# The fifth key piece: a DMA transpose on ScalarE's queue in place of a load, five TensorE transposes and a copy

## The chip, the core and the metric

The kernel runs on one core of one Trainium2 chip. The metric is the device time of one execution in microseconds (us); lower is better. Three executions of the kernel before took 236.49, 236.51 and 236.56 us.

## The reference

The kernel computes one transformer block on x of 1 x 2048 tokens x 640 channels, all in bf16: a linear attention with a learned feature map (32 heads of 20 channels), then a feed-forward layer of 1728 hidden channels. Both have a layer norm ahead of them and a residual around them.

```python
qkv = (x @ wqkv) -> q, k, v                       # x here is layernorm(x)
pq = einsum("bhsd,hdf->bhsf", q, w_phi)           # pk likewise, from k
phi_k = concat(softmax(pk), softmax(-pk))         # phi_q likewise
kv = einsum("bhsf,bhsd->bhfd", phi_k, v);  z = sum_s phi_k
o = einsum(phi_q, kv) / (einsum(phi_q, z) + 1e-6)
h = x + o @ wo
h2 = h + silu(layernorm(h) @ w1) @ w2
```

## The kernel before, in words

The 2048 tokens are 16 tiles of 128. Weights stay in on-chip memory; the 640 input channels are five pieces of 128 rows (C = 5).

The kernel never computes k and then pk. It folds the key weights and `w_phi` into one matrix `Wfk` (640 x 640) first, so that one projection gives pk. Folding contracts over the output channels of the key weights, so TensorE needs their transpose `wTk`, piece by piece. For each piece c of the key weights, before the change:

- `lk` loads it (128 rows x 640 columns, 160 KB) into `wk[:, c]` (the DMA is issued at L236, in the helper `dma`);
- `wt.c` (L322) transposes its five 128 x 128 blocks on TensorE into one bank of PSUM;
- `wc.c` copies them to `wTk` (L171 on ScalarE for pieces 0 and 1, L169 on VectorE for pieces 2, 3 and 4);
- `fk.c` (L337) multiplies that piece of `wTk` by `phb`, the block-diagonal form of `w_phi`, in six matmuls;
- `fc.c` (L171, a cast) copies the result to `Wfk[:, c]` on ScalarE.

Beside this, the first tiles of x are made ready. `st` (L273, L274) takes mean and variance on VectorE; `rs` (L278 on VectorE, then L281 and L283 on GpSimd) turns the variance into a reciprocal root, L281 being the power; `xn` (L297) normalizes on VectorE; `xt` (L308) transposes on TensorE and `xc` copies the result to `XnT`. Then `kp.0` (L370), the first projection by `Wfk`, starts the long row of matmuls that lasts to the end.

Before the first key piece is there, TensorE runs matmuls on constants (`wm`, L268): eight of 512 columns ahead of `wt.0`, six of 256 columns between `wt.0` and `wt.1`.

The order on every engine is written out by hand in one long string, `ORDER`: each word calls one operation, and each engine runs its instructions in the order of the words. A letter `s` behind a load puts the DMA on SyncE's queue, `a` on ScalarE's, `@n` names the PSUM bank. The loads of the key pieces 0 to 3 are on SyncE's queue, that of piece 4 is the third and last DMA on ScalarE's queue, behind x tile 0 and `w_phi`. The completion semaphores of the DMAs go round among eight; a DMA that gets a semaphore again waits on its queue until the DMA that had it before has landed. Here the load of x tiles 4 to 7 (`lx.4.8`, on SyncE's queue) gets the semaphore of piece 4.

The kernel already holds DMA transposes: `xd`, `td` and `hd` (L315, L559, L630) move normalized tiles through them, and `lq` (L251) brings the five pieces of the query weights in transposed from DRAM, all on SyncE's queue. The first of these is issued 16.37 us after the start.

Of the kernel before, what the change touches and what calls it, by code (L numbers as in the profile page):

```python
# [22 lines left out]
WHERE = {t: (g, i) for g, ts in enumerate(GROUPS) for i, t in enumerate(ts)}  # L23

ORDER = """
mk mo lx.0.1.a lk.0.1.s lp.a lx.1.2.s lk.4.5.a wm.512@7 wm.512@7 wm.512@7 wm.512@7 wm.512@7 wm.512@7
wm.512@7 wm.512@7 wt.0@0 lk.1.2.s ta wc.0.a wm.256@2 wm.256@2 wm.256@2 wm.256@2 wm.256@2 wm.256@2 wt.1@1 wc.1.a st.0 rs.0.1
ph.v fk.0@2 fc.0.a st.1 lk.2.3.s wt.2@4 wc.2.v lk.3.4.s wt.3@5 wc.3.v fk.1@6 fc.1.a rs.1.2 fk.2@0 fc.2.a
lx.2.4.s xn.0.v lx.8.12.s wt.4@4 wc.4.v lv.0.3.s fk.3@2 fc.3.a xt.0@5 xn.1.v xc.0.v st.2 fk.4@6 fc.4.a
rs.2.3 lv.3.5.s mc.0 xt.1@4 xc.1.a st.9 st.8 rs.8.10 lx.4.8.s st.3 rs.3.4 kp.0@0 ke.0 xn.2.a kp.1@2 ke.1  # L30
lx.12.16.s vp.1@6 st.10 xt.2@5 vp.0@0 xc.2.a xn.9.a vc.0.a vp.2@2 st.11 lo.2.5.s xn.3.v xt.3@4 xc.3.a
rs.10.12 xn.8.a vc.2.a vc.1.a kp.2@0 ke.2 st.4 xd.9 st.5 kp.3@4 lo.0.2.s ke.3 rs.4.6 vp.3@2 xn.11.v vp.9@6
# [38 lines left out]
def kernel(  # L71
# [11 lines left out]
    nc = tc.nc  # L83

    P = nc.NUM_PARTITIONS
    T = 16
    D = 640
# [46 lines left out]
    wTk = first.tile([P, C, D], BF16, name="wTk")  # L134
# [116 lines left out]
        nc.sync.dma_start_transpose(wTq[:, :, c * P : (c + 1) * P], A_wqkv[c * P : (c + 1) * P, 0:D])  # L251

    def op_lt(c, q="s"):
        nc.sync.dma_start_transpose(wTk[:, :, c * P : (c + 1) * P], A_wqkv[c * P : (c + 1) * P, D : 2 * D])

    def op_lo(a, b, q="s"):
        dma(q, wo[:, a:b, :], A_wo[a * P : b * P].rearrange("(c p) n -> p c n", p=P))
# [500 lines left out]
```

## Time and profile before

| | before |
|---|---|
| median of 3 runs | 236.51 us (236.49 to 236.56) |
| profiled execution, whole | 236.35 us |
| its span in the profile | 234.4 us |
| granted TensorE clock | 1.0 |
| TensorE busy | 230.5 us, 98% of the span |
| VectorE / ScalarE / GpSimd busy | 133.5 / 114.5 / 95.4 us |

The span runs from the first to the last instruction that the profiler records; 1.95 us of the profiled execution lie outside it. In the views, PE is TensorE's matmuls and PEld its weight loads, DVE is VectorE, ACT ScalarE, POOL GpSimd, SP SyncE; a "q" behind a name (SPq, ACTq) is the engine's queue of issued DMAs and waits. A row of the timeline gives the start in us, the time that it took in us, the engine, the line of the code, the operation, output<-input, how many, and in brackets the idle time before it and what ended it.

### The profile page before, as it was taken

To read this page: it belongs to the slowest core of one execution; us is meant where nothing else is said; L and a number is where in the kernel's file an instruction comes from. 1 tells how busy PE (TensorE), PEld (TensorE's weight loads), DVE (VectorE), ACT (ScalarE), POOL (GpSimd) and SP (SyncE) were. 2 spreads that over 40 slices of the span, in tenths; PEclk is the share of its full clock that TensorE was granted. 3 is DMA by queue.
4 is the path that set the end of the run, shared out by engine and by line. 5 is a ranking of instruction groups with operands and counts; after the bars stand their busy time and mean duration, and the time that the engine had idled before them with its cause. 6 is when DMAs were issued, how large, how long until landed. Compare 5 with 4: busy or idle time off the path is not lost.

```text
span 234.4 us, 6307 instructions
## 1 busy us (share of the span) xinstructions
PE 230.5 (98%) x2674; PEld 148.4 (63%) x2674; DVE 133.5 (57%) x249; ACT 114.5 (49%) x171; POOL 95.4 (41%) x190
## 2 busy tenths in 40 slices
PE   8999999999999999999999999999999999999995
PEld 4777777776554556876645455556776865566662
DVE  3999999999968899788956641301341310001132
ACT  3789996885857776742244536260040015613000
POOL 7485798997904455765285123141040000000000
PEclk9999999999999999999999999999999999999999
DMA  7967758839101375325823202123212300000112
GB/s 203 381 234 147 82 112 110 182 64 350 37 3 31 59 176 148 59 49 98 142 55 61 56 3 55 30 57 63 88 24 57 106 27 5 0 3 2 54 34 81
DMA packets 44844, 20.67 MB, mean 88 GB/s; under 512 B 34448, under 2 KB 44304, under 8 KB 44816
## 3 DMA queue, kind: packets, MB, share of 16 engines
q1 hardware_dynamic: 43728, 19.88, 36.1%
q10 hardware_dynamic: 1088, 0.39, 0.8%
q8 instruction: 21, 0.34, 0.6%
q14 instruction: 7, 0.06, 0.1%
HBM read 9.61 MB, written 2.62 MB: 52 GB/s over the span
## 4 chain that ended last, share of the span: by engine, by line
PE 98%; ACT 1%; DVE 0%; issue 0%
PE mm L691 24%; PE mm L645 24%; PE mm L370 19%; PE mm L457 10%; PE mm L566 9%; PE mm L504 3%; PE mm L268 2%; PE mm L427 2%; PE mm L337 1%; PE mm L655 1%; PE mm L704 1%; ACT EqT L479 1%; PE mm L322 1%; PE mm L308 0%; DVE ob L721 0%
## 5 line engine op out<-in xcount | busy, mean ns | idle before, releaser
L691 PE MATMUL mm<-w,shT 128*128 128x320 bf16 (+2 forms) x416 | 58.7, 299 | 0.0
L645 PE MATMUL mm<-HnT,w 128*128 128x512 bf16 (+1 forms) x325 | 58.6, 337 | 0.0
L691 PEld LDWEIGHTS <-shT 128*128 128x128 bf16 x416 | 39.6, 98 | 17.2 <-issue 1.1
L667 ACT ACTIVATE shT<-mm 128x1024 bf16<-128x1024 f32 (+2 forms) x29 | 27.6, 963 | 44.6 <-PE mm L645 43.1
L712 DVE TENSOR_TENSOR ob<-mm,X 128x640 bf16<-128x640 f32 x15 | 12.3, 819 | 62.3 <-PE mm L691 59.3
L645 PEld LDWEIGHTS <-w 128*128 128x128 bf16 x325 | 31.4, 98 | 23.2
L370 PEld LDWEIGHTS <-XnT 128*128 128x128 bf16 x320 | 30.8, 98 | 12.0
L414 POOL TENSOR_TENSOR Ek<-Ek,Sk 128x1280 bf16<-128x1280 bf16 (+2 forms) x15 | 32.9, 2217 | 4.0 <-DVE Sk L406 4.0
L539 POOL TENSOR_TENSOR o<-u,rd 128x320 bf16<-128x320 f32 x28 | 19.9, 727 | 22.9 <-DVE rd L533 16.4
L583 ACT ACTIVATE sq<-X 128x640 bf16<-128x640 bf16 x16 | 11.7, 732 | 28.3 <-DVE X L575 27.2
L566 PE MATMUL mm<-wo,ot 128*128 128x320 bf16 x160 | 23.9, 299 | 0.3 <-ACT EqT L479 0.3
L457 PE MATMUL mm<-XnT,Wfq 128*128 128x512 bf16 x100 | 23.8, 380 | 0.0
L370 PE MATMUL mm<-wv,XnT 128*128 128x320 bf16 x160 | 23.7, 299 | 0.0
L370 PE MATMUL mm<-Wfk,XnT 128*128 128x320 bf16 x160 | 23.5, 299 | 0.0
L395 ACT ACTIVATE Ek<-mm 128x640 bf16<-128x640 f32 x32 | 20.5, 714 | 6.0 <-PE mm L370 5.1
L403 DVE TENSOR_REDUCE Sk<-Ek 128x64 f32<-128x1280 bf16 x16 | 23.2, 1452 | 0.3 <-ACT Ek L395 0.3
L479 ACT ACTIVATE EqT<-mm 128x1024 bf16<-128x1024 f32 (+1 forms) x24 | 19.7, 879 | 4.9 <-PE mm L457 4.8
L575 DVE SCALAR_TENSOR_TENSOR X<-mm,X 128x640 bf16<-128x640 f32 x16 | 13.0, 818 | 15.4 <-PE mm L566 15.1
L566 PEld LDWEIGHTS <-ot 128*128 128x128 bf16 x160 | 15.7, 98 | 7.3 <-issue 0.2
L273 DVE BATCH_NORM_STATS2 stats<-X 128x6 f32<-128x320 bf16 x32 | 13.6, 467 | 3.8 <-DMA X<-in_A_x_dram 3.8
L457 PEld LDWEIGHTS <-Wfq 128*128 128x128 bf16 x100 | 9.1, 98 | 9.3
L525 DVE TENSOR_TENSOR u<-mm,w 128x672 f32<-128x672 f32 x16 | 13.7, 857 | 1.2 <-DVE w L523 0.3
(78 smaller groups left out, 204.3 us busy)
## 6 DMA issues: line engine op xcount, KB each, us to landing
out_dram<-ob SPq DMA_DIRECT2D x15, 160.0 KB, 1.8
w<-in_B_w_dram SPq DMA_DIRECT2D x6, 360.0 KB, 4.5
X<-in_A_x_dram SPq DMA_DIRECT2D x3, 640.0 KB, 7.8
w<-in_B_w_dram SPq DMA_DIRECT2D x5, 320.0 KB, 5.8
wk<-in_A_wqkv_dram SPq DMA_DIRECT2D x4, 160.0 KB, 4.2
wv<-in_A_wqkv_dram SPq DMA_DIRECT2D x1, 480.0 KB, 6.4
wo<-in_A_wo_dram SPq DMA_DIRECT2D x1, 480.0 KB, 9.7
w<-in_B_w_dram SPq DMA_DIRECT2D x1, 480.0 KB, 4.6
```

The lines of the kernel that those rows point to most:

```text
L370: nc.tensor.matmul(ps[:, half, 0:320], tok(XnT[t // GT], t)[:, c, :], W[:, c, half * 320 : (half + 1) * 320], start=(c == 0), stop=(c == C ...
L395: nc.scalar.activation(Ek[:, s, :].rearrange("p (a n) -> p a n", a=2), tl["kp", t][:, :, 0:320], AF.Exp, scale=1.0 - 2.0 * s,)
L403: nc.vector.tensor_reduce(Sk[:], tl["ek", t][:].rearrange("p s (h f) -> p (s h) f", f=DH), axis=AX.X, op=ALU.add,)
L414: nc.gpsimd.tensor_tensor(Ek3[:, 0:n], Ek3[:, 0:n], Sk[:, 0:n].unsqueeze(2).to_broadcast([P, n, DH]), op=ALU.mult,)
L457: nc.tensor.matmul(tl["qp", g, i][:, k, :], Wfq[:, c, r * P : (r + 1) * P], XnT[g][:, c, :], start=(c == 0), stop=(c == C - 1),)
L479: nc.scalar.activation(E[:, s, rs[0] : rs[-1] + 1, :], tl["qp", g, i][:, 0 : len(rs), :], AF.Exp, scale=1.0 - 2.0 * s,)
L525: nc.vector.tensor_tensor(u[:], A[1][:, :, :, 0:21], w[:].unsqueeze(3).to_broadcast([P, 4, 8, 21]), op=ALU.mult,)
L539: (nc.vector if eng == "v" else nc.gpsimd).tensor_tensor(tl["o", t][:, a * 320 : (a + 1) * 320].rearrange("p (h f) -> p h f", f=DH), tl["u ...
L566: nc.tensor.matmul(ps[:, half, 0:320], tl["ot", t][:, c, :], wo[:, c, half * 320 : (half + 1) * 320], start=(c == 0), stop=(c == C - 1),)
L645: nc.tensor.matmul(ps[:, i * W : (i + 1) * W], w1[:, c, fc * P : (fc + 1) * P], HnT[g][:, c, 0:W], start=(c == 0), stop=(c == C - 1), skip ...
L667: nc.scalar.activation(sh[:, a:b], tl["up", g, k][:, 0 : b - a], AF.Silu)
L691: nc.tensor.matmul(ps, shT[g][:, fc * W + i * P : fc * W + (i + 1) * P], w2[:, fc, a:b], start=first and fc == 0, stop=last and fc == FC - ...
```

## The change

Piece 4 is no longer loaded into `wk`. A DMA transpose on ScalarE's queue, at the place of the former load, writes its transpose from DRAM straight into `wTk`. The load of the piece, its five transposes on TensorE (`wt.4`) and its copy on VectorE (`wc.4`) go. `op_lt` was in the kernel before, but no word of `ORDER` called it; it now takes the queue. Everything else keeps its place: `fk.4` stands where it did, now waiting for the DMA in place of the copy.

```diff
-mk mo lx.0.1.a lk.0.1.s lp.a lx.1.2.s lk.4.5.a wm.512@7 wm.512@7 ...
+mk mo lx.0.1.a lk.0.1.s lp.a lx.1.2.s lt.4.a wm.512@7 wm.512@7 ...
...
-lx.2.4.s xn.0.v lx.8.12.s wt.4@4 wc.4.v lv.0.3.s fk.3@2 fc.3.a xt.0@5 xn.1.v xc.0.v st.2 fk.4@6 fc.4.a
+lx.2.4.s xn.0.v lx.8.12.s lv.0.3.s fk.3@2 fc.3.a xt.0@5 xn.1.v xc.0.v st.2 fk.4@6 fc.4.a
...
     def op_lt(c, q="s"):
-        nc.sync.dma_start_transpose(wTk[:, :, c * P : (c + 1) * P], A_wqkv[c * P : (c + 1) * P, D : 2 * D])
+        (nc.sync if q == "s" else nc.scalar).dma_start_transpose(wTk[:, :, c * P : (c + 1) * P], A_wqkv[c * P : (c + 1) * P, D : 2 * D])
```

Engine by engine: TensorE has ten rows fewer (five weight loads, five transposes), VectorE one copy fewer, ScalarE a transposing DMA issue in place of a plain one. The instructions of GpSimd and SyncE and their order are the same.

More of the change, by code (lines that the diff above doesn't have):

```diff
@@ L25 @@
 ORDER = """
-mk mo lx.0.1.a lk.0.1.s lp.a lx.1.2.s lk.4.5.a wm.512@7 wm.512@7 wm.512@7 wm.512@7 wm.512@7 wm.512@7
+mk mo lx.0.1.a lk.0.1.s lp.a lx.1.2.s lt.4.a wm.512@7 wm.512@7 wm.512@7 wm.512@7 wm.512@7 wm.512@7
 wm.512@7 wm.512@7 wt.0@0 lk.1.2.s ta wc.0.a wm.256@2 wm.256@2 wm.256@2 wm.256@2 wm.256@2 wm.256@2 wt.1@1 wc.1.a st.0 rs.0.1
 ph.v fk.0@2 fc.0.a st.1 lk.2.3.s wt.2@4 wc.2.v lk.3.4.s wt.3@5 wc.3.v fk.1@6 fc.1.a rs.1.2 fk.2@0 fc.2.a
-lx.2.4.s xn.0.v lx.8.12.s wt.4@4 wc.4.v lv.0.3.s fk.3@2 fc.3.a xt.0@5 xn.1.v xc.0.v st.2 fk.4@6 fc.4.a
+lx.2.4.s xn.0.v lx.8.12.s lv.0.3.s fk.3@2 fc.3.a xt.0@5 xn.1.v xc.0.v st.2 fk.4@6 fc.4.a
 rs.2.3 lv.3.5.s mc.0 xt.1@4 xc.1.a st.9 st.8 rs.8.10 lx.4.8.s st.3 rs.3.4 kp.0@0 ke.0 xn.2.a kp.1@2 ke.1
```

## The prediction

> **What bounds the kernel now.** I read the page's busy times and its chain first, then TensorE's waits, then the chain of the first 25 us, and last the timeline and the DMA landings of that stretch.
>
> ```profile
> PE 230.5 (98%) x2674; PEld 148.4 (63%) x2674; DVE 133.5 (57%) x249; ACT 114.5 (49%) x171; POOL 95.4 (41%) x190
> PE 98%; ACT 1%; DVE 0%; issue 0%
> PE mm L566 <- ACT EqT L479: 0.3, 1, 0.3
> ```
>
> TensorE is the bound from end to end: 98% busy, 98% of the chain, and once started its one long wait is 0.3 us. Little can absorb a shift of its row of matmuls, so what counts is when that row begins: the first projection, L370. The chain ahead of it:
>
> ```profile
> 6.25 0.45 PE mm L322 x5
> 6.70 0.32 PE mm L337 x6
> 7.02 0.56 PE mm L322 x10
> 7.58 0.80 PE mm L337 x12
> 8.37 0.28 PE mm L322 x5
> 8.65 0.32 PE mm L337 x6
> 8.96 0.28 PE mm L308 x5
> 9.24 0.48 PE mm L337 x6
> 9.72 0.32 PE mm L308 x5
> 10.04 4.19 PE mm L370 x30
> ```
>
> The chain is drawn as TensorE alone, because its modelled ends touch. The five transposes that the change removes stand in it at 8.37 with 0.28 us. Whether they are worth that much, the timeline tells: it shows which waits end just before TensorE's steps.
>
> ```profile
> 6.25 0.28 PEld L322 LDWEIGHTS <-wk 128*128 128x128 bf16 x5 [0.51 <-DMA wk<-in_A_wqkv_dram]
> 6.80 0.60 PEld L322 LDWEIGHTS <-wk 128*128 128x128 bf16 x10
> 7.33 0.89 DVE L169 COPY wTk<-mm 128x640 bf16<-128x640 bf16 x2 [0.22 <-PE mm L322]
> 8.14 0.14 DVE L278 TENSOR_SCALAR RS<-MV 128x1 f32<-128x1 f32 x1
> 8.37 0.67 POOL L281 TENSOR_TENSOR RS<-RS,nhalf 128x1 f32<-128x1 f32 x1 [1.52 <-DVE RS L278]
> 8.69 0.49 DVE L169 COPY wTk<-mm 128x640 bf16<-128x640 bf16 x1
> 9.10 0.44 DVE L297 TENSOR_SCALAR xn<-X,MV,RS 128x640 bf16<-128x640 bf16 x1
> 9.23 0.31 PEld L337 LDWEIGHTS <-wTk 128*128 128x128 bf16 x6 [0.16 <-DVE wTk L169]
> 9.45 0.48 DVE L169 COPY XnT<-mm 128x640 bf16<-128x640 bf16 x1
> 9.98 3.92 PEld L370 LDWEIGHTS <-XnT 128*128 128x128 bf16 x30
> ```
>
> Read backwards. The projection begins at 9.98, right after VectorE's copy of the first transposed tile (9.45 + 0.48 = 9.93). In program order that copy stands behind the second normalization (9.10). This one needs the power on GpSimd, which ends at 8.37 + 0.67 = 9.04. The power needs L278 at 8.14, which stands behind the copies of pieces 2 and 3 (7.33), these wait for piece 2's transposes on TensorE (weights from 6.80), and those run behind piece 1's, which wait for a DMA until 6.25. So the stretch from 6.25 to 9.98 hangs on the landing of key piece 1 and then runs through VectorE and GpSimd; from 8.2 on TensorE only looks like the bound.
>
> **What goes.** Five transposes (0.28 us) and the copy of 0.49 us, with TensorE's wait of 0.16 us for that copy. On the face of it 0.28 + 0.16 = 0.44 us of TensorE. But with the copy gone VectorE is free from 8.69 on and then stands still until the power ends at 9.04; the normalization can start at 9.04 at the earliest, not 9.10. The gain lies between 0 and 0.06 us; I take 0.03, since a semaphore has to pass between. The rest of the 0.44 us turns into idle TensorE: what hides it is GpSimd's power, and if the power were done early the whole 0.44 us would come out. Behind the projection VectorE's order is unchanged, so nothing else is freed.
>
> **What is added on ScalarE.** The issue of the DMA.
>
> ```profile
> 1.70 0.56 ACTq L236 DMA_DIRECT2D wk<-in_A_wqkv_dram  x1
> 2.28 1.28 ACT L264 ACT_TABLE_LOAD   x1 [2.28 <-issue]
> 4.97 0.69 ACT L171 COPY wTk<-mm 128x640 bf16<-128x640 bf16 x1 [1.20 <-PE mm L322]
> 6.54 0.48 PE L337 MATMUL mm<-phb,wTk 128*128 128x140 bf16 x6
> 21.71 1.23 SPq L251 DMA_TRANSPOSE wk<-in_A_wqkv_dram  x1
> ```
>
> A transpose takes 1.23 us to issue on SyncE's queue (the nearest row; the trace has none on ScalarE's), a load 0.56: 0.67 more. Behind it on ScalarE wait the table load and piece 0's copy. The table load moves to 2.95 and ends at 4.23; the copy stays at 4.97, because 1.20 us of idle time precede the copy. Even if the issue took as long again, the copy would be done by 6.5, when the first fold at 6.54 wants it. Cost 0.
>
> **When the transposed piece lands.** The first folding matmul of piece 4 is wanted at 9.23: that is how late it can be without moving the projection.
>
> ```profile
> phr<-in_A_w_phi_dram ACTq DMA_DIRECT2D x1, 25.0 KB, 3.6
> wk<-in_A_wqkv_dram ACTq DMA_DIRECT2D x1, 160.0 KB, 4.3
> wk<-in_A_wqkv_dram SPq DMA_DIRECT2D x1, 160.0 KB, 4.5
> DMA to landing us min/median/max: 2.8/3.1/4.2
> 22.80:24.20 1.40, 1.40 (x13) 1.02 (x11) 1.36 (x4) 1.22 (x2) 0.04 (x1) 1.00 0.53 117
> 5.00:7.00 2.00, 1.97 (x20) 1.31 (x19) 1.97 (x5) 0.93 (x2) 1.50 (x2) 1.00 1.14 399
> ```
>
> The third row is key piece 1, the fourth the five DMA transposes of L251, the last two are windows whose last columns are the share of the 16 DMA engines and the rate. Piece 4's load landed at 1.70 + 4.3 = 6.0. The window 22.8 to 24.2 holds the data of one such transpose and nothing else (117 GB/s over 1.40 us, its 160 KB): 0.53 x 1.40 = 0.74 us of all engines. In the window 5 to 7, plain rows took 1.14 us of engine time for each 399 KB, so 0.47 us for 160 KB. The transpose keeps the engines 0.27 us longer; sharing them half and half with SyncE's queue, it lands 0.5 us later than the load, at 6.5, and with the slowest against the fastest row (4.2 - 2.8 = 1.4 us) at 7.9. Both are well before 9.23. Cost 0.
>
> SyncE's queue is passed too: the load of x tiles 4 to 7 waits for piece 4's semaphore.
>
> ```profile
> 5.98 1.11 SPq L236 DMA_DIRECT2D X<-in_A_x_dram  x2
> X<-in_A_x_dram SPq DMA_DIRECT2D x1, 640.0 KB, 7.8
> 16.62 0.88 DVE L273 BATCH_NORM_STATS2 stats<-X 128x6 f32<-128x320 bf16 x2
> ```
>
> It was issued at 5.98, landed at 13.8 and is first read at 16.62, so a landing of piece 4 even at 7.9 (1.9 us later) is covered by 2.8 us, and the load of x tiles 12 to 15 and that of `wo` move with it. Cost 0.
>
> **What moves for the other key pieces.** This is the term that decides. Piece 1 landed at 1.74 + 4.5 = 6.24, just after piece 4's load at 6.0, and the two shared the engines. Now piece 1 shares them with a transpose, which occupies them 0.27 us longer and can go ahead or behind. Nothing in the trace of before shows a transpose on one queue beside loads on the other, so bounds: if the transpose goes ahead whole, pieces 1 to 3 land 0.27 us later and the chain moves by 0.27. If it goes out behind them, or in small parts between them, piece 1 lands earlier by up to the 0.47 us that the load took from it; but the chain gains at most 0.22, the idle time that VectorE has before the copies at 7.33. If the queues take equal turns, piece 1 shares with as much of the transpose as of the load before and lands as before; only pieces 2 and 3 come later, by up to 0.27 us, and the 0.28 us of removed transposes that stood behind them on TensorE make room for that. I take 0 as the middle of the two ends.
>
> A page of the Trainium skill bears on this term: "Advanced Engine Details and Errata", section "X-Bar Transpose (TRN2)", states that transpose DMAs are as fast as regular ones. By that rule the term would be 0 from the upper end as well. The two windows above differ from it: 0.74 us of engine time against 0.47 for the same bytes.
>
> **The sum.** -0.03 (copy) + 0 (ScalarE) + 0 (landing, SyncE) + 0 (other pieces, from -0.22 to +0.27) = -0.03 us on the profiled execution's 236.35 us. The median of the three runs is 0.16 us above that execution; the change is laid on the median: 236.51 - 0.03 = 236.5 us, by the bounds of the terms from 236.2 to 236.8. A measurement of this kernel can tell about 0.2%, 0.47 us, from no change, so faster means below 236.04 and slower above 236.98: the forecast is no change.
>
> **Rival 1, slower: the transpose's issue holds up SyncE's loads.** Piece 4's DMA is issued at 1.70 and piece 1's at 1.74, side by side on two queues. If what makes the descriptors serves one queue at a time, the 0.67 us by which the transpose's issue is longer fall on pieces 1 to 3, and with them on the chain: 236.51 + 0.67 = 237.2, up to 0.9 with the 0.27 us of engine time on top (237.4). It counts as slower from the point at which piece 1 lands after 6.24 + 0.47 = 6.71. For it: the row of three SyncE issues below takes 0.50 us each while ScalarE issues too, the row of two later ones, when ScalarE issues none, 0.47. Against it: that difference is small. Chance 0.22.
>
> ```profile
> 1.74 1.49 SPq L236 DMA_DIRECT2D wk<-in_A_wqkv_dram  x3
> 4.88 0.93 SPq L236 DMA_DIRECT2D wv<-in_A_wqkv_dram  x2
> ```
>
> **Rival 2, slower: the piece lands too late.** From a landing at 9.2 on, every further delay moves the projection; for a slower verdict it takes 9.7. The nearest rows argue against it: that would be 8.0 us from issue, against at most 4.2 for the transposes and 4.5 for the loads of this stretch. A landing at 10.2 would give 236.51 + 1.0 = 237.5. Chance 0.06.
>
> A rule points this way: "VectorE: DVE Perf Modes", section "The three transpose paths", of the Trainium skill gives 390 ns for a 128 x 128 block on TensorE and 1309 ns by DMA, and its rules prefer TensorE. As an estimate from that page, five blocks one after the other would take 6.5 us and land at 8.2; the trace does not agree, with five blocks landing in 2.8 to 4.2 us from issue.
>
> **Rival 3, faster: both gates open.** GpSimd's spans are rough. If the power is really done well before 9.04, the 0.44 us of TensorE come out, and if piece 1 also lands early, another 0.22 us: 236.51 - 0.66 = 235.85. Either alone stays within what can't be told from no change. For it: the second normalization begins as the copy ends (8.69 + 0.49, the rows overlapping by 0.08). Against it: 9.04 and 9.10 fit a semaphore's way too well. Chance 0.08.
>
> **How the numbers follow.** Forecast 0.64, all of it within 0.2%; rivals 1 and 2 together 0.28 slower; rival 3 0.08 faster. The range takes the forecast's own 236.2 to 236.8 and the lower end of rival 1, to 237.2; left out are rival 2, rival 3 and the upper part of rival 1, under 2 in 10.
>
> **What would show it.** Right: the projection at 9.9 to 10.0, the normalization before it still released by L281, a gap on TensorE ahead of the second tile's transposes (L308), piece 4 landed at 6 to 8. Rival 1: the weight load of piece 1 at 6.7 or later, behind a DMA. Rival 2: the last L337 group waiting for the transpose beyond 9.2. Rival 3: L370 at 9.5 or before. The forecast is wrong if the projection keeps its time and the end does not, since I let the start carry the whole shift.

## The result, and the profile after

The changed kernel is slower: 237.22 us against 236.49 us (medians of 15 runs each), ratio 1.0039 with a 95% interval of 1.0021 to 1.0056. The forecast of 236.5 us and no change was wrong, and the upper end of its range, 237.2, was just passed. Three of the 15 runs stand apart at 238.64 to 238.77 us, with a granted TensorE clock of 0.993 in place of 1.0; without them the median is 237.18 us.

The profiled execution took 237.33 us with a span of 235.6 us, 1.2 more than before. TensorE's busy time hardly changed (ten rows fewer); its one long wait behind the start is 0.3 us as before:

```profile
PE 229.8 (98%) x2669; PEld 147.5 (63%) x2669; DVE 133.1 (57%) x248; ACT 114.6 (49%) x171; POOL 95.4 (40%) x190
PE 93%; DMA 2%; DVE 1%; ACT 1%; SPq 1%; POOL 0%; issue 0%
```

The chain has a DMA in it now, which it had not before. Its first 25 us show where:

```profile
2.19 5.80 DMA wk<-in_A_wqkv_dram
7.99 0.05 issue
8.04 0.47 PE mm L322 x5
8.50 0.02 issue
8.53 0.91 DVE wTk L169 x2
9.44 0.07 DVE RS L278
9.51 0.07 issue
9.58 0.68 POOL RS L281
10.26 0.03 issue
10.28 0.46 DVE xn L297
10.74 0.05 issue
10.79 0.45 PE mm L308 x5
11.24 4.20 PE mm L370 x30
```

From the copies of pieces 2 and 3 on it is step for step the chain that the prediction read in the profile before: the copies, L278, the power, the second normalization, the projection. Only its head differs. The DMA at 2.19 is key piece 2: 5.8 us from issue to landing, at 7.99. In the kernel before, its weight load at 6.80 waited for nothing. The timeline with the releasers:

```profile
1.72 1.30 ACTq L254 DMA_TRANSPOSE wTk<-in_A_wqkv_dram  x1
1.72 1.37 SPq L236 DMA_DIRECT2D wk<-in_A_wqkv_dram  x3
6.01 0.28 PEld L322 LDWEIGHTS <-wk 128*128 128x128 bf16 x5 [0.98 <-DMA wk<-in_A_wqkv_dram]
8.03 0.70 PEld L322 LDWEIGHTS <-wk 128*128 128x128 bf16 x10 [1.09 <-DMA wk<-in_A_wqkv_dram]
10.28 0.45 DVE L297 TENSOR_SCALAR xn<-X,MV,RS 128x640 bf16<-128x640 bf16 x1 [0.43 <-POOL RS L281]
11.18 3.78 PEld L370 LDWEIGHTS <-XnT 128*128 128x128 bf16 x29
```

Piece 1 came a little earlier than before (6.01 against 6.25), pieces 2 and 3 came 1.2 us late, and the projection began at 11.18 in place of 9.98: the whole 1.2 us of the span. Behind it the rows of VectorE and ScalarE stand 1.20 us later than before, all the way to the end. SyncE's three issues took 1.37 us beside the transpose's issue, before the change 1.49, so the issue did not hold them up.

What happened on the DMA engines is in one window, 4 to 8 us. The last two columns are the share of the 16 engines and the rate in GB/s. The kernel before:

```profile
4.00:8.00 4.00, 3.97 (x41) 2.97 (x41) 3.68 (x10) 1.95 (x3) 1.98 (x6) 1.00 1.07 373
```

The changed kernel:

```profile
4.00:8.00 4.00, 2.20 (x23) 1.42 (x22) 3.18 (x8) 2.58 (x5) 1.99 (x6) 1.00 1.10 229
```

The engines count as busy as before and move 39% less. In those 4 us 576 kB fewer arrived. Alone, in the quiet window of the prediction, a transpose had cost 0.74 us of the engines; here loads and transpose are slow together (the transpose took 6.1 us from issue to landing). Four profiles show this same start, the others being those of e7, e9 and e12 below, whose edits leave the DMAs as they are: the window moved 229, 191, 258 and 208 GB/s, and the projection began between 10.97 and 11.67. So a rate from one profile is good to some 30 GB/s.

### The profile page after: what moved, and what is told of

It reads as the page before. It is cut to its first block, busy times and chain, and to the rows that moved or that the text cites. A ratio compares the mean times of both kernels' runs of the same rounds, so it can differ in the third digit from the quotient of the medians.

```text
span 235.6 us, 6296 instructions
## 1 busy us (share of the span) xinstructions
PE 229.8 (98%) x2669; PEld 147.5 (63%) x2669; DVE 133.1 (57%) x248; ACT 114.6 (49%) x171; POOL 95.4 (40%) x190
## 4 chain that ended last, share of the span: by engine, by line
PE 93%; DMA 2%; DVE 1%; ACT 1%; SPq 1%; POOL 0%; issue 0%
PE mm L645 24%; PE mm L691 24%; PE mm L370 19%; PE mm L457 10%; PE mm L566 9%; PE mm L504 3%; DMA wk<-in_A_wqkv_dram 2%; PE mm L427 2%; PE mm L655 1%; PE mm L704 1%; ACT EqT L479 1%; PE mm L337 1%; SPq L236 1%; PE mm L308 0%; DVE ob L721 0%; DVE wTk L169 0%
```

## The experiments

Three theories stood at first. Mixing: a DMA transpose in flight while loads are in flight slows both far beyond its own engine time. Packets: its 640 packets of 256 bytes do it, transposed or not. Issue: its long issue on ScalarE holds up SyncE's loads. Each row below has its ratio to runs of the kernel before on the same chip, whose medians stand in the rows "before"; "outside" is the time of an execution less its span. All but the ratio are medians in us.

| run | time | span | outside | ratio to before |
|---|---|---|---|---|
| before (as run with e1 to e4) | 236.52 | 234.5 | 1.95 | |
| before (as run with e5 to e8) | 236.44 | 234.5 | 1.95 | |
| before (as run with e9, e10) | 236.38 | 234.4 | 1.98 | |
| before (as run with e11, e12) | 236.40 | 234.5 | 1.97 | |
| changed (before: 236.49) | 237.22 | 235.5 | 1.73 | 1.0039 (1.0021 to 1.0056) |
| e1 no piece 4 | 236.24 | 234.5 | 1.76 | 0.9986 (0.9977 to 0.9994) |
| e2 plain, 256 bytes | 236.06 | 234.3 | 1.75 | 0.9980 (0.9971 to 0.9989) |
| e3 SyncE, behind | 236.58 | 234.8 | 1.72 | 0.9999 (0.9984 to 1.0015) |
| e4 added alone | 237.35 | 235.3 | 2.05 | 1.0033 (1.0021 to 1.0045) |
| e5 two blocks | 236.29 | 234.6 | 1.72 | 0.9992 (0.9983 to 1.0001) |
| e6 load behind | 236.43 | 234.5 | 1.95 | 1.0007 (0.9995 to 1.0019) |
| e7 filled | 237.14 | 235.45 | 1.72 | 1.0034 (1.0021 to 1.0046) |
| e8 two pieces | 237.73 | 235.95 | 1.75 | 1.0053 (1.0036 to 1.0069) |
| e9 two memsets | 237.28 | 235.35 | 1.93 | 1.0050 (1.0034 to 1.0066) |
| e10 split | 236.04 | 234.3 | 1.70 | 0.9990 (0.9982 to 0.9999) |
| e11 later | 236.14 | 234.4 | 1.74 | 0.9987 (0.9978 to 0.9996) |
| e12 work back | 237.22 | 235.3 | 1.96 | 1.0044 (1.0032 to 1.0057) |

**e1, no DMA for piece 4.**

```diff
-... lx.1.2.s lt.4.a wm.512@7 ...
+... lx.1.2.s wm.512@7 ...
+        cw = 3 if ce == 4 and key == "fk" else ce     # fk.4 reads piece 3
...
-                    wT[:, r, ce * P : (ce + 1) * P],
+                    wT[:, r, cw * P : (cw + 1) * P],
```

> Changed kernel with no DMA for piece 4 at all; the fold of piece 4 reads piece 3's transpose, so the result is not the reference's. Theories: (mixing) a DMA transpose in flight on one queue beside loads on the other slows both far beyond its own engine time; (packets) its 640 packets of 256 bytes do it, transposed or not; (issue) its long issue on ScalarE holds up SyncE's loads. By all three the delay goes with the DMA: key pieces 1 to 3 land by 6.0, 6.3 and 6.8 us, the projection starts at 9.7 to 9.95, 236.2 to 236.5 us. If the time stays near 237.2, the delay comes from what was removed, not from the DMA.

Measured 236.24 us; in its profile the projection begins at 9.84. The delay goes with the DMA. (With one DMA fewer the semaphores move on by one place too, and x tiles 2 and 3 are issued at 3.25 in place of 4.35; e2 keeps the number of DMAs.) But the gain over the kernel before is not in the span (234.5 for both); it lies outside it, which none of the theories had foreseen. e9 takes this up.

**e2, the same packets without transposing.**

```diff
-        (... nc.scalar).dma_start_transpose(wTk[:, :, c * P : (c + 1) * P], A_wqkv[c * P : (c + 1) * P, D : 2 * D])
+        dma(q, wTk[:, :, c * P : (c + 1) * P], A_wqkv[c * P : (c + 1) * P, D : 2 * D].rearrange("p (r k) -> p r k", r=C))
```

> Piece 4 on ScalarE's queue as a plain load cut into the same 640 packets of 256 bytes, with no transposing (it writes piece 4 untransposed into the transposed tile, so the result is not the reference's). Mixing: no slowing, pieces 2 and 3 land at 6.3 to 7.1 us, projection at 9.8 to 10.1, 236.3 to 236.7 us. Packets: as the changed kernel, pieces 2 and 3 at about 8.0 and 8.5, projection at 11.2, 237.2 us. Issue: a plain issue of about 0.6 us, so no slowing either.

Measured 236.06 us, 0.2% faster than before, with the projection at 9.82. Its profile in the same window, and the start of the projection:

```profile
4.00:8.00 4.00, 3.81 (x45) 2.88 (x43) 3.87 (x11) 2.08 (x4) 1.99 (x6) 1.00 1.06 335
9.82 3.24 PEld L370 LDWEIGHTS <-XnT 128*128 128x128 bf16 x25
```

Same queue, same place, same bytes, same rows of 256 bytes: 335 GB/s against 229. The theory of packets falls. What remains is the transposing or its long issue, which e5 tells apart. The difference in this window is (335 - 229) x 4 = 424 kB, 1.3 us at 335 GB/s; by the four profiles of the changed start it is 0.9 to 1.7 us.

The traces list every DMA packet with its queue, size and time, and show where this goes. Piece 4's 640 packets of 256 bytes take 18 ns each in e2, 0.72 us of all engines, which is what a transpose took in the prediction's quiet window (18 ns, 0.74 us). In the changed kernel they take 27 ns in the mean, 1.09 us. Most of the loss is the neighbours': SyncE's first 640 packets of 1280 bytes (key pieces 0 to 3 and x tile 1) take 87 ns in the mean against 65, 3.49 us of all engines against 2.61. In both kernels the median stays at 55 ns; 33 packets take over 300 ns, in e2 four.

**e3, the transpose on SyncE's queue behind piece 3.**

```diff
-... lx.1.2.s lt.4.a ...      lk.3.4.s wt.3@5 ...
+... lx.1.2.s ...             lk.3.4.s lt.4.s wt.3@5 ...
```

> The same DMA transpose, moved to SyncE's queue right behind key piece 3, so that no other queue has loads beside it. Mixing: pieces 1 to 3 land by 6.0, 6.3 and 6.8 us, the transpose itself takes its 0.74 us of engines and lands at 7 to 8, projection at 9.7 to 10.0, 236.2 to 236.5 us. Packets: pieces on time, but the transpose still drags, landing after 8.5, with x tiles 2 and 3 behind it after 9.5. Issue: pieces on time, x tiles 2 and 3 issued 0.7 us later than before; time as before.

The key pieces came on time and the projection began at 9.83, as expected, but the time did not follow: 236.58 us, spread from 235.78 to 237.38. The profile of a run at 237.13 us shows what took the gain back:

```profile
7.21 1.41 PE L337 MATMUL mm<-phb,wTk 128*128 128x140 bf16 x18
9.83 2.69 PEld L370 LDWEIGHTS <-XnT 128*128 128x128 bf16 x21
13.63 1.60 PE L370 MATMUL mm<-wv,XnT 128*128 128x320 bf16 x10 [0.91 <-DMA wv<-in_A_wqkv_dram]
```

The value weights came 0.9 us late. (VectorE waited for x tiles 2 and 3 as well, 0.92 us.) With no loads on another queue, the transpose still drags on the loads that follow it on its own; "on the other queue" in the theory of mixing was too narrow.

**e4, the transpose added to the kernel before.**

```diff
-... lx.1.2.s lk.4.5.a wm.512@7 ...
+... lx.1.2.s lk.4.5.a lt.4.a wm.512@7 ...
```

> Kernel before with the DMA transpose of piece 4 added on ScalarE's queue behind the load of piece 4; the five TensorE transposes and the copy stay and write the same values over it. Mixing and packets: pieces 2 and 3 land 1 to 2 us later than in the kernel before, projection at 11.0 to 11.7, 237.2 to 237.9 us; the difference to the changed kernel is what the removed work is worth, 0 to 0.45 us. Issue: the same sign, 0.5 to 0.9 us slower than before, with SyncE's issues of pieces 1 to 3 visibly stretched.

The time, 237.35 us, is in the expected range, and it proves little: with one DMA more, piece 3's load is the ninth and gets the semaphore of x tile 0, so its issue waited for that to land.

```profile
1.73 2.73 SPq L236 DMA_DIRECT2D wk<-in_A_wqkv_dram  x3
6.68 0.33 PEld L322 LDWEIGHTS <-wk 128*128 128x128 bf16 x5
8.06 0.28 PEld L322 LDWEIGHTS <-wk 128*128 128x128 bf16 x5 [1.06 <-DMA wk<-in_A_wqkv_dram]
4.00:8.00 4.00, 3.18 (x28) 2.39 (x27) 3.53 (x9) 2.97 (x5) 1.98 (x6) 1.00 1.13 327
```

Piece 2 came on time (6.68) and piece 3 alone was late. Adding a DMA to a ring of eight semaphores moved a wait; e12 asks for the worth of the removed work without one. One thing e4 does show: a transpose of the same piece is in flight here beside loads, it landed 4.6 us from its issue, and the window moved 327 GB/s, nearly e2's 335. Here its data moved late, from 5.3 to 6.3 us, behind piece 4's plain load and with one key load fewer beside it. So not every transpose beside loads costs what it cost in the changed kernel; which of these differences spares it is not shown.

**e5, two of the five blocks.**

```diff
-... wTk[:, :, c * P : (c + 1) * P], A_wqkv[c * P : (c + 1) * P, D : 2 * D])
+... wTk[:, 0:2, c * P : (c + 1) * P], A_wqkv[c * P : (c + 1) * P, D : D + 2 * P])
...
-                    wT[:, r, ce * P : (ce + 1) * P],
+                    wT[:, r, (3 if key == "fk" and ce == 4 and r >= 2 else ce) * P :][:, 0:P],
```

> Changed kernel with the DMA transpose cut to two of its five blocks (256 of 640 packets); the fold of piece 4 reads piece 3's blocks for the other three, so the result is not the reference's. Mixing with a cost per packet (the loads lose engine time as long as the transpose is in flight): piece 2 lands 0.3 to 0.8 us later than with no transpose instead of 1.7 us, projection at 10.0 to 10.5, 236.3 to 236.8 us. Mixing with a fixed cost (a change of mode, once for each transpose): pieces 2 and 3 as late as in the changed kernel, projection at 10.9 or later, 237.0 us or more.

**e8, two pieces.**

```diff
-... lx.1.2.s lt.4.a ...         lk.3.4.s wt.3@5 wc.3.v fk.1@6 ...
+... lx.1.2.s lt.4.a lt.3.a ...  fk.1@6 ...
```

> The suspected cost doubled: pieces 3 and 4 both come by DMA transposes, one behind the other on ScalarE's queue, and piece 3's load, TensorE transposes and copy go too. Mixing with a cost per packet: the loads on SyncE's queue stay slow for twice as long, x tiles 1 to 3 and the value weights come late too, projection at 11.5 to 13, 238 to 239.5 us. Mixing with a fixed cost or none for the second transpose: about as the changed kernel, 237.0 to 237.5 us, since piece 3's load no longer has to wait in line.

The two were meant as a scale. Window and start of the projection in e5, then in e8:

```profile
4.00:8.00 4.00, 3.79 (x37) 2.66 (x36) 3.36 (x9) 2.38 (x5) 1.99 (x6) 1.00 1.08 277
10.39 2.69 PEld L370 LDWEIGHTS <-XnT 128*128 128x128 bf16 x21
```

```profile
4.00:8.00 4.00, 3.09 (x24) 2.03 (x24) 3.18 (x8) 3.28 (x5) 1.99 (x6) 1.00 1.19 177
10.70 1.20 PEld L370 LDWEIGHTS <-XnT 128*128 128x128 bf16 x10
```

e5 came out as the theory with a cost per packet said: 236.29 us, projection at 10.39. From none to two to five blocks (e2, e5, changed) the projection begins at 9.82, 10.39 and 11.18, and the time is 236.06, 236.29 and 237.22 us: the amount counts. (The profile of e5 is that of its slowest run.) It is not the issue: that of the two blocks in e5 took nearly as long as that of five,

```profile
1.72 1.25 ACTq L254 DMA_TRANSPOSE wTk<-in_A_wqkv_dram  x1
```

and the time is a full 0.9 us lower. With e8 the scale ends. It came out at 237.73 us, below the 238 to 239.5 expected; its projection began at 10.70, before the changed kernel's, with one load fewer in the line, and its profile fell back by 0.6 us against the changed kernel's between 60 and 70 us, where no key piece is involved. So twice the transposes did not cost the start twice. The packets do not grow evenly either: SyncE's packets of 1280 bytes take 87 ns in the mean with two blocks, 87 with five and 96 with ten (512 packets there, one load fewer), against 65 with none. A cost that comes once for each transpose is thus not ruled out beside one that grows with its size.

**e6, the plain load moved behind piece 3.**

```diff
-... lx.1.2.s lk.4.5.a ...      lk.3.4.s wt.3@5 ...
+... lx.1.2.s ...               lk.3.4.s lk.4.5.s wt.3@5 ...
```

> Kernel before with piece 4's plain load moved from ScalarE's queue to SyncE's, right behind piece 3; nothing else changed. If the order of the key pieces on the DMA engines sets the start (as the run without piece 4 suggests), pieces 1 to 3 land about 0.3 us earlier, the projection starts at 9.75 to 9.9, 236.1 to 236.4 us: better than both kernels. If the gain of the run without piece 4 came from the removed TensorE transposes and the copy instead, no gain here: 236.4 to 236.7 us.

236.43 us, no gain (0.9995 to 1.0019). The median span is 234.5 us, that of e1 and of the kernel before: the order of the key pieces' loads was not what made e1 fast. The profiled run was the slowest, 237.57 us, and carries a warning:

```profile
7.53 0.70 PEld L322 LDWEIGHTS <-wk 128*128 128x128 bf16 x10 [0.54 <-DMA wk<-in_A_wqkv_dram]
4.00:8.00 4.00, 3.64 (x29) 2.78 (x29) 3.18 (x8) 1.91 (x3) 1.99 (x6) 1.00 0.96 256
```

With plain loads alone pieces 2 and 3 came late here, and the window moved 256 GB/s. A low rate in one profile is no proof of a transpose; that the changed kernel is slower by transposing rests on the medians of e1, e2 and e5.

**e7, TensorE's wait filled.**

```diff
-st.1 lk.2.3.s wt.2@4 ...
+st.1 lk.2.3.s wm.256@7 (eight times) wt.2@4 ...
```

> Changed kernel with eight more matmuls of 256 columns on constants between the first fold and piece 2's transposes, where TensorE now waits for the DMA. If the runs of the changed kernel at 238.7 us and a granted clock of 0.993 come from TensorE's idle time there, none of these runs shows 0.993, and the median stays at 237.0 to 237.3 us, as the landing of piece 2 is unchanged. If they have another cause, about one in five stays at 238.7.

The median did not move, and none of its six runs shows a clock of 0.993. At three in 15, six runs without one come about in one case of four. None of the eleven runs of e9 and e12 shows it either, and these keep TensorE's gaps. So the three runs of the changed kernel stay unexplained.

**e9, two memsets more on VectorE.**

```diff
+    def op_dz():
+        nc.vector.memset(nhalf[:, 3:4], -0.5)
-... yp.14.0@2 ...
+... dz dz yp.14.0@2 ...
```

> Changed kernel with two tiny memsets more on VectorE, late, where VectorE is idle; the result does not change. In all runs so far the part of the execution outside the profiled span is 1.95 to 2.05 us in the kernels that keep the copy of piece 4 (before, the added transpose, the moved load) and 1.72 to 1.76 in those without it, also in the one with eight more matmuls. If the number of VectorE's instructions sets it, it goes back to 1.9 or more here and the median rises by 0.2 to about 237.4 us; if it is something else of the removed steps, it stays at 1.7 and the median at 237.2 us.

Outside the span it took 1.93 us in place of 1.73. The two memsets run at 193 us on an idle VectorE, 59 ns each:

```profile
L206 DVE MEMSET nhalf<- x2: 59/59/59, 193.1 to 193.2; 128x1 f32 x2
```

So 0.2 us outside the span go with VectorE's instructions: it is 1.93 to 2.05 us in every kernel that has the copy of piece 4 or the memsets, 1.70 to 1.76 in every one that has not, eight more matmuls (e7) or not. It is not so much for each: e8, with one copy fewer still, has 1.75.

**e12, the removed work put back.**

```diff
-... lx.8.12.s lv.0.3.s fk.3@2 ...
+... lx.8.12.s wt.4@4 wc.4.v lv.0.3.s fk.3@2 ...     # wt.4 on piece 3, wc.4 into Wfq, overwritten later
```

> Changed kernel with the removed work put back as a dummy: five TensorE transposes (of piece 3 again) and a copy on VectorE into a tile that is overwritten later, at the old place; the result does not change, and no DMA is added. The prediction's step that the removed work is worth 0 to 0.06 us on the chain: the span stays at 235.5 us. The face value of 0.44 us: the span rises to about 235.9 us. Outside the span 1.9 to 2.0 us in place of 1.73, by the number of VectorE's instructions, so the median is 237.4 by the first and 237.9 us by the second.

The span's median is 235.3 us against the changed kernel's 235.5: the five transposes and the copy cost nothing on the chain that these runs can tell. The profile shows why; the rows are the power, the dummy copy and the second normalization:

```profile
9.78 0.67 POOL L281 TENSOR_TENSOR RS<-RS,nhalf 128x1 f32<-128x1 f32 x1 [2.94 <-DVE RS L278]
10.10 0.49 DVE L169 COPY Wfq<-mm 128x640 bf16<-128x640 bf16 x1
10.51 0.44 DVE L297 TENSOR_SCALAR xn<-X,MV,RS 128x640 bf16<-128x640 bf16 x1
```

With the copy in the way the normalization starts 0.06 us after the power's end (10.51 - 10.45), in the changed kernel 0.03 (10.28 - 10.25). Outside the span it is 1.96 us, as expected. The time is the changed kernel's 237.22 us.

**e10 and e11, a place for the transpose.** From e3 it was clear which load had to come sooner.

```diff
 # e10, against e3
-lx.2.4.s xn.0.v lx.8.12.s lv.0.3.s ... lv.3.5.s mc.0 ...
+lx.2.4.s xn.0.v lx.8.10.s lv.0.3.s ... lv.3.5.s lx.10.12.s mc.0 ...
 # e11, against e10
-lk.3.4.s lt.4.s wt.3@5 ... lx.2.4.s xn.0.v ...
+lk.3.4.s wt.3@5 ... lx.2.4.s lt.4.s xn.0.v ...
```

> The DMA transpose on SyncE's queue behind key piece 3, and the load of x tiles 8 to 11 cut in two, the second half behind the value weights. Without the cut, projections began at 9.83 us, but the value weights came at 13.6 us, 0.9 us late, and the runs spread from 235.78 to 237.38. If the transpose's drag on the loads behind it is about 1 us of DMA work and slack can take it, the value weights land by 12.7, the spread goes and the median is 235.8 to 236.1 us, better than both kernels. If the drag is larger or falls on another load (x tiles 8 and 9, wanted at 10.9), it stays at 236.3 to 236.8 us.

> As the split kernel, but the DMA transpose stands one load later on SyncE's queue, behind x tiles 2 and 3. There the transpose landed at 7.1 us and x tiles 2 and 3 at 10.3, 0.5 us too late for VectorE. If the transpose drags what is behind it, x tiles 2 and 3 now land by 8.5, the transpose at 8 to 8.8, just in time for its fold at 8.8, and the median is 235.8 to 236.0 us. If it lands later, the fold waits and the projection moves by as much: 236.1 to 236.6 us.

e10 runs at 236.04 us (235.91 to 236.47 us over 11 runs), 0.1% faster than the kernel before by its ratio, just clear of no change, where the changed kernel is 0.4% slower. TensorE no longer waits for the value weights; VectorE still waits for x tiles 2 and 3, 0.54 us:

```profile
9.81 3.96 PEld L370 LDWEIGHTS <-XnT 128*128 128x128 bf16 x30
10.30 0.89 DVE L273 BATCH_NORM_STATS2 stats<-X 128x6 f32<-128x320 bf16 x2 [0.54 <-DMA X<-in_A_x_dram]
12.54 1.57 PE L370 MATMUL mm<-wv,XnT 128*128 128x320 bf16 x10
```

e11 removes that wait (statistics at 9.92), but its projection begins at 10.06, and it comes to the same, 236.14 us. Both are faster than the two kernels; between them the runs do not choose. But their gain over the kernel before is hardly on the chain: the median spans are 234.3 and 234.4 us against 234.4 and 234.5 on the same chips, and outside the span they take 1.70 and 1.74 us against 1.98 and 1.97.

## Why the prediction was wrong, step by step

**What bounds the kernel: right.** The start of the projection carried the shift: 11.18 - 9.98 = 1.20 us, the rows behind it keep it, and the span grew by 1.2.

**What goes, 0 to 0.06 us: right.** The second normalization is released by the power in the profile after (0.43 us of waiting), and e12 finds nothing on the span for the removed work; the two profiles differ by 0.03 us at that step. Rival 3, in which both gates open, is out: the power ends at 10.25 and the normalization starts at 10.28.

**ScalarE's issue, 0: right.** It took 1.30 us, and the copy of piece 0 came at 4.68, even earlier than before (4.97).

**Landing of piece 4, 6.5 to 7.9: right, in part by luck.** It landed at 1.72 + 6.1 = 7.8, before the 9.23 at which it was wanted, but at the far end of the range, and that end was a spread taken without its reason. SyncE's later load did wait for it, without harm.

**The other key pieces, -0.22 to +0.27 us: wrong, and this is the whole miss.** Piece 1 did come 0.24 us earlier, as the prediction allowed for a transpose that goes out behind it. Pieces 2 and 3 came 1.2 us later than wanted, where the prediction allowed at most 0.27. The step that failed is the price: 0.74 us of engine time was read from a window in which the transpose was alone, and taken as what it costs beside loads. The 0.27 us by which this exceeds a load is the price of small packets, for e2's plain ones took 0.72 us. What transposing cost beside loads, e2 against the changed kernel, is 1.3 us of DMA time in this window (0.9 to 1.7), most of it in the packets of the other loads, which the prediction took as unchanged. The rule of the Trainium skill that the prediction weighed ("Advanced Engine Details and Errata", section "X-Bar Transpose (TRN2)": as fast as regular DMAs) is further off still: with the same bytes in the same place the window moved 335 GB/s with the plain load, 229 with the transpose.

The profile before held a warning that was passed over. The prediction used the slowest transpose of L251, 4.2 us to landing against 2.8, as mere spread. ("At most 4.2 for the transposes" holds for L251; one of L315 took 4.4.) In the window 40 to 41, which holds its data, and in another one like it, the share of the engines stands far above 1 at a low rate:

```profile
27.00:28.00 1.00, 1.00 (x10) 0.73 (x8) 0.96 (x3) 1.00 (x2) 0.83 (x3) 1.00 2.62 129
40.00:41.00 1.00, 1.00 (x10) 0.72 (x8) 1.00 (x3) 1.00 (x3) 1.00 (x2) 1.00 2.18 127
```

All packets of loads and transposes that start in these windows are a transpose's, of 256 bytes; they take 83 and 70 ns in the mean, up to 1.7 us, against 18 in the quiet window. Beside them the trace lists one packet of 16 KB of instructions on another queue in each, from 26.88 and from 39.66, for 1.5 us. These were the rows nearest to a transpose in company, and not the quiet window at 22.8.

**Rival 1, the issue: its sign and time came true, its mechanism did not.** It gave 237.2 us, by coincidence: SyncE's issues were no longer than before, and e5 has the long issue without the loss.

**Outside the span: a term the sum did not have.** The median span rose by 1.0 us (234.5 to 235.5), the time outside fell by 0.22 (1.95 to 1.73): 0.78, against 0.73 measured. The prediction took what lies around the span as fixed.

Not settled: why a transpose slows loads, and when it does not (e4); no run here shows the engines one by one. Nor is it shown how much of the cost comes once for each transpose, or what the three runs at a clock of 0.993 come from.

## What to carry to other kernels

Price a DMA transpose by a row where other transfers are in flight; its time alone says little about what it does to a start full of loads, where the other loads pay most of it. Before taking work off an engine, find what ends last just behind that work: here the five transposes stood in the drawn chain with 0.28 us and were worth nothing on the span. Compare medians, and read one profile's rate with its spread in mind, as e6 shows. If a transpose must run early, put it behind the last load that is urgent and look again at every deadline after it, as e10 did; here that only won back the start.

## What the runs showed that was not expected

- A DMA transpose beside loads cut the rate of all DMA in a window of 4 us from 335 GB/s to 229 (191 to 258 over four profiles), with the engines' share near 1.1 in all; its own 256-byte packets rose from 18 to 27 ns in the mean, the other loads' packets of 1280 bytes from 65 to 87. In e4, where its data moved later, the window kept 327.
- Two instructions of 59 ns on an idle VectorE changed the time outside the span from 1.73 to 1.93 us, as the removed copy had changed it from 1.95 to 1.73.
- One more DMA at the start made an unrelated load's issue wait some 1.4 us for a semaphore (e4: 2.73 us for three issues, 1.37 in the changed kernel).
